# A gated mix of softmax attention and memory attention: the factors of the octets are made by GpSimd with a power and a Newton step instead of by VectorE's reciprocal

## Chip, cores and metric

One Trainium2 chip, one core. The metric is the device time of one execution in microseconds (us). The kernel before took 1857.35 us, the median of three runs (1856.53 to 1861.13).

## What is computed

Two attentions over the same 2048 rows of 512, with 32 heads of 16, mixed by a gate that depends on the row. A is full softmax attention. B works in four segments of 512 rows: causal softmax inside a segment, and a linear memory (a matrix M and a vector z for each head) that holds the segments before.

```python
def reference(A_x, A_wqkv, A_wo, B_x, B_wq, B_wk, B_wv, B_wo, B_beta, gate_w):
    # A
    scores = jnp.einsum("bhqd,bhkd->bhqk", q, k) * scale
    p = _softmax(scores, axis=-1)
    o = jnp.einsum("bhqk,bhkd->bhqd", p, v)
    a = o.transpose(...).reshape(B, S, D) @ wo
    # B, for each segment s
    logits = jnp.einsum("bhqd,bhkd->bhqk", qs, ks) * scale + mask
    a_dot = jnp.einsum("bhqk,bhkd->bhqd", _softmax(logits, axis=-1), vs)
    num = jnp.einsum("bhld,bhde->bhle", pq, M)
    den = jnp.einsum("bhld,bhd->bhl", pq, z)[..., None] + 1e-6
    o = g * (num / den) + (1.0 - g) * a_dot
    M = M + jnp.einsum("bhld,bhle->bhde", pk, vs)
    z = z + jnp.einsum("bhld->bhd", pk)
    # mix
    g = _sigmoid((x * gate_w).sum(-1, keepdims=True))
    return g * a + (1 - g) * b
```

## The kernel before

A first stage, some 330 us long, projects queries, keys and values of both sides, stores them in DRAM, makes the memory parts of B (numerators `numd`, denominators `dend`) and begins the maxima. The main loop that follows is the place of the change.

The work of the main loop is cut into units. A unit is one side, a group of four heads (`g`, eight groups) and a chunk of 512 queries (`c`, four chunks). An A unit takes 64 slots and a B unit 10; the two kinds alternate, so that a pair takes 74 rounds of the loop, and in what follows "a unit" is such a pair of 74 rounds. One round `n` does this, in the order in which it is written, which is the order on every engine:

- things due at this round (`at`, `beside`): loads, and the steps of the octets
- `score_part(n)` (line 640): one 50x128 by 50x512 product of keys and queries on TensorE into one of three PSUM banks `st`, and its exponential on ScalarE (line 663) into `p`. The diagonal blocks of B are zeroed by GpSimd (line 644).
- `max_part(n + 96)`: the same kind of product (line 196) for a slot 96 rounds ahead, into one of four PSUM banks `sm`, and the maximum over its 512 keys on VectorE (line 211; for B with a mask, line 221, one or two pieces). When a unit's maxima are complete, GpSimd splits them into two parts `ms` (lines 178 and 179), TensorE transposes those eight to twelve rounds later (line 187), and SyncE puts them beside the queries (line 193), where the score product subtracts them.
- every third round: products of `p` and the values (line 696, up to three pieces of 128 queries, four or five when the queue of pieces is long) into the bank `ops`, or, for finished chunks, sixteen output products at a time (line 773).

With the values a column of ones is multiplied, so that row 16 of each head's result is the softmax sum. A finished unit is stored to DRAM (`od`, line 701). When two units of a side are stored, their eight heads are an octet, and `octet` divides them by their sums and multiplies them by the gate. Its four steps are due at rounds `t0`, `t0 + 10`, `t0 + 17` and `t0 + 28`:

- `load`: SyncE fetches the 8 x 512 sums as a tile `rec` of 128x32 (line 737) and the values (line 744).
- `factors`: VectorE makes the reciprocal (line 747) and multiplies it by the gate (line 751), for side B also by one less the memory's share `ogh` in the same instruction (line 749). SyncE sends the 128x32 factors to DRAM (line 752).
- `factor`: SyncE fetches them back, spread over the 16 dims of each head, as `inv` of 128x512 (line 756).
- `scale`: GpSimd multiplies the values by `inv` (line 759), and for B from the second chunk on adds the scaled memory part (line 761).

There are three kinds of octets: A and B (16 each), and M, the memory part of B (12, from the second chunk on), whose sums are `dend`. The last octet, A of the last chunk, is handled after the loop with `vector=True`: its scale is VectorE's, since everything waits for it. The instructions of SyncE, GpSimd and VectorE run in the order of the program, each engine waiting by itself.

Of the kernel before, what the change touches and what calls it, by code (L numbers as in the profile page):

```python
# [10 lines left out]
F32 = mybir.dt.float32  # L11
F32R = mybir.dt.float32r
AF = mybir.ActivationFunctionType
ALU = mybir.AluOpType
# [31 lines left out]
def gated_mix(ctx, tc, x, xT, wqkv, a_wo, b_wq, b_wk, b_wv, b_wo, beta, gate_w, out):  # L46
    nc = tc.nc
# [35 lines left out]
    ogh = const.tile([128, NO], F32, name="ogh")  # L83
# [26 lines left out]
    for k in range(NU):  # L110
# [4 lines left out]
        for p in range(64 + 10 * len(bs)):  # L115
            r = (len(maxs) + 1) % 2
# [456 lines left out]
    gate = {(s, c): gp.tile([128, 32], F32, name=f"g{s}{c}") for s in "AB" for c in range(NCH)}  # L573
# [6 lines left out]
    fr = ctx.enter_context(tc.tile_pool(name="fr", bufs=1, reuse_waits="tile"))  # L580
# [132 lines left out]
    def heads(rows):  # L713

        return rows.unsqueeze(0).broadcast_to([DH, 8, CH])

    held = {}
    scaled = set()

# [3 lines left out]
    def at(n, f):  # L723
        beside.setdefault(n, []).append(f)

    def octet(side, o, c, t0, vector=False):

        hs = slice(8 * o, 8 * o + 8)
        sums, rows, eng = (dend[c][hs], rdM[c][hs], nc.gpsimd) if side == "M" else (od[side, c][hs, 16], rd[side, c][hs], nc.gpsimd)
        if vector:  # L730
            eng = nc.vector
        k = {}

        def load():
            assert side == "M" or {(side, 2 * o, c), (side, 2 * o + 1, c)} <= stored
            k["rec"] = fr.tile([128, 32], F32, tag="rec", name="rec", bufs=3)
            nc.sync.dma_start(k["rec"], sums.rearrange("h (q t) -> h q t", q=16))
            if side == "M":
                k["v"] = held["M", c, o] = fr.tile([128, CH], F32, tag="vM", name="vM", bufs=2)
            else:  # L740
                if (side, c) not in held:
                    held[side, c] = fr.tile([128, NO, CH], F32, tag="v" + side, name="v" + side, bufs=2)
                k["v"] = held[side, c][:, o]
            nc.sync.dma_start(k["v"], numd[c][:, o] if side == "M" else od[side, c][hs, 0:16].rearrange("h r t -> r h t"))

        def factors():
            nc.vector.reciprocal(k["rec"], k["rec"])  # L747
            if side == "B":
                nc.vector.scalar_tensor_tensor(k["rec"], k["rec"], ogh[:, o:o + 1], gate["B", c], op0=ALU.mult, op1=ALU.mult)
            else:  # L750
                nc.vector.tensor_mul(k["rec"], k["rec"], gate["A" if side == "A" else "B", c])
            nc.sync.dma_start(rows.rearrange("h (q t) -> (h q) t", q=16), k["rec"])

        def factor():
            k["inv"] = fr.tile([128, CH], F32, tag="inv", name="inv", bufs=3)
            nc.sync.dma_start(k["inv"], heads(rows))

        def scale():
            eng.tensor_mul(k["v"], k["v"], k["inv"])
            if side == "B" and c:  # L760
                eng.tensor_add(k["v"], k["v"], held.pop(("M", c, o)))
            scaled.add((side, o, c))
        for n, f in ((0, load), (10, factors), (17, factor), (28, scale)):
            if t0 is None:
                f()
            else:
                at(t0 + n, f)
# [113 lines left out]
    for b in range(4):  # L881
# [3 lines left out]
        t = fr.tile([128, D], F32, tag="vM" if b % 2 else "res", name="res", bufs=2)  # L885
# [4 lines left out]
def build():  # L890
    import concourse.bacc as bacc
    nc = bacc.Bacc("TRN2", target_bir_lowering=False, num_devices=1)
    shapes = {"x": (S, D), "xT": (D, S), "wqkv": (D, 3 * D), "a_wo": (D, D), "b_wq": (D, D), "b_wk": (D, D),
              "b_wv": (D, D), "b_wo": (D, D), "beta": (H,), "gate_w": (D,)}
    args = [nc.dram_tensor(n, s, F32, kind="ExternalInput").ap() for n, s in shapes.items()]
    out = nc.dram_tensor("out", (S, D), F32, kind="ExternalOutput").ap()
    with tile.TileContext(nc) as tc:
        gated_mix(tc, *args, out)
    return nc
# [23 lines left out]
```

## Time and profile before

| | |
|---|---|
| median of three runs | 1857.35 us |
| the profiled execution | 1856.77 us, span 1855.0 us |
| TensorE, matmul rows | 1846.4 us, 17769 instructions |
| VectorE | 1609.3 us (87% of the span), 3417 instructions |
| ScalarE | 1446.3 us (78%) |
| GpSimd | 236.6 us (13%), 387 instructions |
| granted TensorE clock | 1.000 |

In the profile PE is TensorE's matmul, PEld its weight load, DVE VectorE, ACT ScalarE, POOL GpSimd, SPq the queue of SyncE, which issues most DMAs. A group's row holds the line, engine, operation, output<-inputs, shapes and count; after the bar the busy time and the mean ns of one; after the second bar the engine's idle time just before, and what ended it. A row of the order of time holds start, length, engine, line, operation, and in brackets the idle time before it and what ended it. A row of the waits holds who waited for whom, the total in us, how often, and the longest.

### The profile page before, as it was taken

How to read it: one execution, taken by the hardware profiler on the slowest of the kernel's cores; microseconds unless marked ns; L12 is line 12 of the kernel's file. 1: busy time of each engine (PE TensorE's matmuls, PEld its weight loads, DVE VectorE, ACT ScalarE, POOL GpSimd, SP SyncE). 2: the span in 40 equal slices, each digit the busy share in tenths (PEclk: the TensorE clock that was granted, in tenths of full speed). 3: DMA queues.
4: the chain of work that ended last, by engine and by line, in shares of the span. 5: the costliest groups of instructions: out<-in, count | busy, mean ns of one | idle time of the engine just before them, and what ended most of it. 6: DMA issues, size and time to landing. Idle time of an engine off the chain costs nothing.

```text
span 1855.0 us, 45914 instructions
## 1 busy us (share of the span) xinstructions
PE 1846.4 (100%) x17769; PEld 987.1 (53%) x17769; DVE 1609.3 (87%) x3417; ACT 1446.3 (78%) x2772; POOL 236.6 (13%) x387
## 2 busy tenths in 40 slices
PE   9999999999999999999999999999999999999999
PEld 7888676555555554444444444444444455555446
DVE  4234678999999999999999999999999999999920
ACT  5445444888888888888888888888888888888884
POOL 3001222001010101010101010101010100111120
PEclk9999999999999999999999999999999999999999
DMA  7568645345343433454434343434343433433321
GB/s 238 191 232 257 203 170 189 116 110 135 88 112 88 113 88 112 103 115 103 115 99 117 100 111 104 113 103 115 103 115 103 115 105 99 117 102 97 93 65 48
DMA packets 124169, 227.28 MB, mean 123 GB/s; under 512 B 34952, under 2 KB 49960, under 8 KB 123440
## 3 DMA queue, kind: packets, MB, share of 16 engines
q1 hardware_dynamic: 122448, 222.68, 42.6%
q8 instruction: 141, 2.31, 0.5%
q0 software_dynamic: 1216, 1.14, 0.2%
q14 instruction: 76, 0.62, 0.1%
q10 hardware_dynamic: 288, 0.52, 0.1%
HBM read 155.52 MB, written 67.52 MB: 120 GB/s over the span
## 4 chain that ended last, share of the span: by engine, by line
PE 94%; DVE 2%; DMA 1%; ACT 1%; POOL 1%; issue 0%; SPq 0%; POOLq 0%; DVEq 0%
PE ops L696 32%; PE st L640 28%; PE sm L196 15%; PE pr L294 11%; PE ops L773 6%; PE sm L773 1%; DVE pm L211 1%; POOL mn L354 1%; PE num L476 1%; DMA raw<-xT 0%; PE mt_ps L187 0%; DMA qdB<-q 0%; PE mps L507 0%; DMA raw<-wqkv 0%; ACT ex L361 0%
## 5 line engine op out<-in xcount | busy, mean ns | idle before, releaser
L663 ACT ACTIVATE p<-st 128x512 f32<-128x512 f32 x2304 | 1210.8, 601 | 207.0 <-PE sm L196 164.4
L211 DVE TENSOR_REDUCE pm<-sm 128x1 f32<-128x512 f32 x2048 | 1264.5, 682 | 14.3 <-PE sm L196 13.7
L196 PE MATMUL sm<-kA,qA 48*128 48x512 f32 x2048 | 737.6, 446 | 0.2 <-DVE pm L211 0.2
L640 PE MATMUL st<-qA,kA 50*128 50x512 f32 x2048 | 678.8, 433 | 0.0
L640 PEld LDWEIGHTS st<-qA,kA 50*128 50x128 f32 x2048 | 334.1, 185 | 423.8 <-ACT p L663 367.8
L696 PE MATMUL ops<-p,vA 128*17 128x512 f32 (+3 forms) x5848 | 556.4, 469 | 0.0
L196 PEld LDWEIGHTS sm<-kA,qA 48*128 48x128 f32 x2048 | 332.9, 184 | 29.6 <-DVE pm L211 11.0
L221 DVE CUSTOM_DVE_ANT_0 rest<-sm,mask 128x128 f32<-128x128 f32 (+3 forms) x512 | 248.3, 485 | 7.5 <-PE sm L196 0.8
L696 PEld LDWEIGHTS ops<-p,vA 128*17 128x17 f32 x5848 | 109.7, 95 | 180.9 <-issue 163.2
L196 PE MATMUL sm<-kB,qB 48*128 48x128 f32 (+3 forms) x512 | 149.3, 352 | 0.0
L644 POOL TENSOR_SCALAR_AFFINE_SELECT p<-p 128x512 f32<-128x512 f32 x128 | 79.5, 637 | 465.4 <-ACT p L663 461.1
L357 DVE TENSOR_TENSOR q<-full,q 128x512 fp32r<-128x512 f32 x64 | 44.4, 694 | 88.3 <-ACT q L350 87.5
L640 PE MATMUL st<-qB,kB 50*128 50x384 f32 (+3 forms) x512 | 114.1, 337 | 0.0
L640 PEld LDWEIGHTS st<-qB,kB 50*128 50x128 f32 x512 | 71.6, 185 | 60.8 <-ACT p L663 56.7
L196 PEld LDWEIGHTS sm<-kB,qB 48*128 48x128 f32 x512 | 86.1, 185 | 7.3 <-DVE pm L211 2.9
L696 PE MATMUL ops<-p,vB 128*17 128x128 f32 (+3 forms) x1192 | 86.5, 398 | 0.0
L349 ACT COPY full<-pr 128x512 f32<-128x512 f32 x64 | 37.4, 584 | 52.5 <-PE pr L294 52.1
L178 POOL CAST ms<-pm 128x16 fp32r<-128x16 f32 x32 | 6.3, 198 | 511.5 <-DVE pm L221 511.5
L747 DVE RECIPROCAL rec<-rec 128x32 f32<-128x32 f32 x44 | 15.2, 344 | 64.7 <-DMA rec<-odA 34.5
L773 PE MATMUL ops<-woA,vA 128*32 128x128 f32 x1664 | 66.9, 278 | 0.0
L773 PE MATMUL ops<-woB,vB 128*32 128x128 f32 x1664 | 64.6, 273 | 0.0
L294 PE MATMUL pr<-xh,wql 128*128 128x512 f32 x128 | 54.4, 425 | 0.3 <-ACT xh L407 0.2
(144 smaller groups left out, 1401.0 us busy)
## 6 DMA issues: line engine op xcount, KB each, us to landing
kA<-kdA SPq DMA_DIRECT2D x256, 128.0 KB
vA<-vdA SPq DMA_DIRECT2D x31, 544.0 KB
kA<-kdA SPq DMA_DIRECT2D x256, 64.0 KB
qdA<-q SPq DMA_DIRECT2D x32, 256.0 KB
kdA<-q SPq DMA_DIRECT2D x32, 256.0 KB
qdB<-q SPq DMA_DIRECT2D x32, 256.0 KB
qA<-qdA SPq DMA_DIRECT2D x64, 128.0 KB
kdB<-q SPq DMA_DIRECT2D x32, 256.0 KB
```

Source lines behind the costliest of these rows:

```text
L196: nc.tensor.matmul(ps[:, n0:n0 + n], rows(qt[u][:, :, s * 128:(s + 1) * 128], h, 48), rows(k[:, :, k0:k0 + n], h, 48), start=True, stop=True)
L211: nc.vector.tensor_reduce(pm[:, h, s, kc:kc + 1], ps, axis=AX.X, op=ALU.max)
L221: nc.vector.tensor_tensor_reduce(out=tri["rest"][:, 0:w], in0=ps[:, n0:n0 + w], in1=tri["mask"][:, CH - w:], scale=-1.0, scalar=3.0e38, op ...
L294: nc.tensor.matmul(ps, l(a, k), r(b, k), start=(n == 0), stop=(n == 11))
L349: nc.scalar.copy(full, ps)
L354: nc.gpsimd.tensor_scalar_min(ph["mn"], full, 0.0)
L357: nc.vector.tensor_sub(q2, full, q1.bitcast(F32))
L640: nc.tensor.matmul(ps[:, n0:n0 + CH - q0], rows(k[:, :, b * 128:(b + 1) * 128], h, 50), rows(q[:, :, q0:], h, 50), start=True, stop=True)
L644: nc.gpsimd.affine_select(out=x, in_=x, pattern=[[0, 4], [1, 128]], base=0, channel_multiplier=-1, compare_op=ALU.is_ge, fill=0.0)
L663: nc.scalar.activation(p[:, h], ps, AF.Exp, scale=SCALE)
L696: nc.tensor.matmul(ops[32 * h:32 * h + 17, q0:q0 + 128 * w], v[:, 17 * h:17 * h + 17], p[:, h, c0:c0 + 128 * w], start=(i == 0), stop=done ...
L773: nc.tensor.matmul(ps[32 * t:32 * t + 32, 128 * (j % (ps.shape[1] // 128)):128 * (j % (ps.shape[1] // 128)) + 128], held[side, c][:, o, 12 ...
```

## The change

For every octet but the last one GpSimd makes the factors: a constant tile `minus` of -1 is set once, `rec` to the power of -1 is taken into `rcp`, and one Newton step corrects it: `err` = 2 - `rec` x `rcp`, `rec` = `rcp` x `err`. Then come the multiplications by `ogh` (B alone, now an instruction of its own) and by the gate. The last octet keeps VectorE's reciprocal and multiplication. Two tiles of 128x32 with two buffers each and the constant are added to the pool `fr`. The rounds at which the steps are due, the DMAs and all other instructions stay as they were.

```diff
+    minus = fr.tile([128, 32], F32, name="minus")
+    nc.gpsimd.memset(minus, -1.0)
     held = {}
     scaled = set()
...
         def factors():
-            nc.vector.reciprocal(k["rec"], k["rec"])
+            rec = k["rec"]
+            if vector:
+                eng.reciprocal(rec, rec)
+            else:
+
+                r, e = (fr.tile([128, 32], F32, tag=t, name=t, bufs=2) for t in ("rcp", "err"))
+                eng.tensor_tensor(r, rec, minus, op=ALU.pow)
+                eng.tensor_mul(e, rec, r)
+                eng.tensor_scalar(e, e, -1.0, 2.0, op0=ALU.mult, op1=ALU.add)
+                eng.tensor_mul(rec, r, e)
             if side == "B":
-                nc.vector.scalar_tensor_tensor(k["rec"], k["rec"], ogh[:, o:o + 1], gate["B", c], op0=ALU.mult, op1=ALU.mult)
-            else:
-                nc.vector.tensor_mul(k["rec"], k["rec"], gate["A" if side == "A" else "B", c])
+                eng.tensor_scalar_mul(rec, rec, ogh[:, o:o + 1])
+            eng.tensor_mul(rec, rec, gate["A" if side == "A" else "B", c])
             nc.sync.dma_start(rows.rearrange("h (q t) -> (h q) t", q=16), k["rec"])
```

## Prediction

> **What bounds the kernel now.** I read the page's head first, for the span against which everything is counted.
>
> ```profile
> span 1855.0 us, 45914 instructions
> ```
>
> TensorE shows as busy all through on that page, but its ends are modelled, so its busy share can't tell whether it works or waits. The next view is the waits, which can.
>
> ```profile
> DVE pm L211 <- PE sm L196: 13.7, 18, 2.4
> ...
> PEld sm L196 <- DVE pm L211: 13.9, 52, 0.6
> ```
>
> In the whole run VectorE stands for a max product 18 times, and TensorE's weight load is seen standing for VectorE's release of a bank 52 times. Both are small, so the two engines run at nearly the same pace, with four banks between them. Which one sets the pace has to be read stage by stage. The kernel offers an experiment of its own: units (74 rounds: 64 of A, 10 of B) alternate between kinds that differ in their octets. In the first chunk the even units hold an A and a B octet, the odd ones none. I put window edges at the starts of the max products that are issued in each unit's first round. Columns: stretch, length, busy time of PE, PEld, DVE, ACT, POOL with counts, clock, DMA.
>
> ```profile
> 420.50:468.30 47.80, 47.59 (x468) 24.19 (x467) 47.25 (x103) 40.57 (x80) 6.18 (x11) 1.00 0.49 132
> 468.30:513.60 45.30, 45.30 (x465) 23.96 (x461) 44.98 (x97) 39.26 (x77) 3.12 (x9) 1.00 0.30 88
> 513.60:561.10 47.50, 47.50 (x462) 24.21 (x461) 47.11 (x102) 40.06 (x79) 5.82 (x11) 1.00 0.41 110
> 561.10:607.60 46.50, 46.50 (x470) 23.67 (x469) 46.19 (x99) 40.55 (x80) 3.59 (x10) 1.00 0.33 90
> 607.60:654.30 46.70, 46.70 (x465) 24.32 (x461) 46.31 (x101) 39.42 (x77) 5.62 (x11) 1.00 0.44 109
> 654.30:700.20 45.90, 45.90 (x461) 23.74 (x460) 45.58 (x98) 39.78 (x78) 3.23 (x9) 1.00 0.33 89
> ```
>
> VectorE is busy all but 0.2 to 0.6 us of each unit, and its busy time follows the length. Three units with octets take 142.0 us, three without 137.7: one pair of octets costs 1.43 us of elapsed time. TensorE's work is the same in both kinds, and its clock is 1.00. So in this stage VectorE is the bound. In the second and third chunks odd units hold one M octet (the memory part), even ones an A and a B octet:
>
> ```profile
> 748.40:794.40 46.00, 46.00 (x442) 20.53 (x438) 45.64 (x99) 39.10 (x78) 4.08 (x9) 1.00 0.38 95
> 794.40:841.60 47.20, 47.20 (x473) 21.52 (x470) 46.81 (x102) 40.61 (x79) 7.41 (x12) 1.00 0.51 113
> 841.60:888.70 47.10, 47.10 (x495) 21.44 (x491) 46.75 (x101) 40.55 (x79) 4.82 (x11) 1.00 0.41 101
> 888.70:935.10 46.40, 46.40 (x442) 21.10 (x438) 46.02 (x101) 39.20 (x78) 6.77 (x11) 1.00 0.48 117
> 935.10:981.90 46.80, 46.80 (x472) 20.97 (x470) 46.45 (x100) 40.59 (x79) 4.77 (x10) 1.00 0.40 100
> 981.90:1029.50 47.60, 47.60 (x497) 21.94 (x493) 47.22 (x103) 40.59 (x79) 7.44 (x13) 1.00 0.50 120
> ```
>
> Sums: 139.9 us with M, 141.2 us with A and B, so 0.43 us a unit for one octet more. In the last chunk units three apart (the same place in the bursts of three rounds) can be compared: the first and third rows hold M, AB; so do the fourth and the second.
>
> ```profile
> 1497.60:1545.70 48.10, 48.10 (x633) 25.22 (x630) 47.09 (x100) 40.90 (x80) 4.88 (x10) 1.00 0.35 100
> 1545.70:1594.20 48.50, 48.50 (x593) 23.84 (x589) 47.50 (x103) 40.86 (x80) 7.41 (x13) 1.00 0.43 120
> ...
> 1641.30:1689.50 48.20, 48.20 (x633) 25.49 (x630) 47.19 (x102) 41.16 (x80) 7.40 (x12) 1.00 0.43 112
> 1689.50:1738.00 48.50, 48.50 (x592) 23.30 (x588) 47.44 (x97) 41.13 (x80) 4.86 (x11) 1.00 0.37 98
> ```
>
> An octet more costs 0.1 us (48.2 against 48.1) and 0.0 (48.5 twice). VectorE idles 1 us a unit here: TensorE, with more value and output products, sets the pace.
>
> **What is removed.** Of 44 octets 43 lose their two VectorE instructions: 16 A less the last, 16 B and 12 M, four of a kind in each chunk and M from the second chunk on.
>
> ```profile
> L747 DVE RECIPROCAL rec<-rec 128x32 f32<-128x32 f32 x44 | 15.2, 344 | 64.7 <-DMA rec<-odA 34.5 <-DMA rec<-dend 23.4 <-DMA rec<-odB 6.9
> L749 DVE SCALAR_TENSOR_TENSOR rec<-rec,ogh,gB 128x32 f32<-128x32 f32 x16 | 4.9, 308 | 0.6
> L751 DVE TENSOR_TENSOR rec<-rec,gA 128x32 f32<-128x32 f32 x16 | 3.1, 192 | 0.5
> ```
>
> Durations overlap, so I take what the pair displaces from the order of time on VectorE:
>
> ```profile
> 991.39 0.34 DVE L747 RECIPROCAL rec<-rec 128x32 f32<-128x32 f32 x1
> 991.76 0.19 DVE L751 TENSOR_TENSOR rec<-rec,gA 128x32 f32<-128x32 f32 x1
> 991.87 1.88 DVE L211 TENSOR_REDUCE pm<-sm 128x1 f32<-128x512 f32 x3
> ```
>
> From 991.39 to 991.87: 0.48 us for A or M, with the next maximum right behind. For B I add the longer second instruction (308 - 192 ns): 0.60 us. A pair A and B is 1.08 us, with an M 1.56 us.
>
> **The sum.** First chunk, four pairs (the last of them falls into the unit after the six shown): 4 x 1.08 = 4.3 us by VectorE's work, 4 x 1.43 = 5.7 us by the units' difference (a burst held by the reciprocals may also starve VectorE afterwards). I take 5.0. Second and third chunk, eight pairs and eight M: the units give back 0.43 us for 0.60 us of work, a share of 0.72; 8 x 1.56 x 0.72 = 9.0 us. Bounds: 12.5 us if every us counts, 0 if TensorE is the bound at the first relief. The share must fall as VectorE's load does, so I take 8.5. Last chunk, three pairs and three M before the maxima end: 4.7 us of work at a share of 0.1, that is 0.5 us (bounds 0 and 4.7). M and B of the last pair come after VectorE's last maximum and hide behind TensorE. Together 14.0 us (bounds 4.3 and 22.9).
>
> **What is added.** GpSimd gets five instructions of 128x32 an octet, six for B, and one constant of -1 at the start. Multiplications are bounded by two rows of its own:
>
> ```profile
> L759 POOL TENSOR_TENSOR vB<-vB,inv 128x512 f32<-128x512 f32 x16 | 20.5, 1283 | 30.9 <-DMA inv<-rdB 30.9
> ...
> L179 POOL TENSOR_TENSOR ms<-pm,ms 128x16 fp32r<-128x16 f32 x32 | 7.1, 223 | 2.6
> ...
> L354 POOL TENSOR_SCALAR mn<-full 128x512 f32<-128x512 f32 x24 | 36.3, 1512 | 102.3 <-ACT full L349 82.0 <-DVE jk L441 20.4
> ```
>
> Between 16 and 512 elements a straight line gives 0.26 us for 32; with a wait for the one before it I count 0.3 us. The power has no row. From below it is 0.26 us, from above by the longest row 1.5 us; being a function and no single step, it is nearer the upper one, and I take 1.5. An A or M octet is then 2.7 us of GpSimd, a B octet 3.0.
>
> This is free only while it hides. The tightest place is a B octet of the second or third chunk; from SyncE's, GpSimd's and TensorE's order of time:
>
> ```profile
> 998.76 0.61 SPq L737 DMA_DIRECT2D rec<-odB  x1
> ```
>
> ```profile
> 1007.64 0.20 POOL L178 CAST ms<-pm 128x16 fp32r<-128x16 f32 x1 [8.36 <-DVE pm L221]
> ```
>
> ```profile
> 1014.18 0.39 PE L187 MATMUL mt_ps<-identf,ms 128*32 128x128 f32 x4
> ```
>
> The sums are fetched at 998.76 and, by the last octet B below, land 2.2 us later, at 1001.0. GpSimd idles from 999.28 to 1007.64, when it must split the maxima, and TensorE needs the split at 1014.18. Queued behind the factors on GpSimd are this split, then the octet's scale; in other octets the diagonals of B. So 6.6 us lie free before the split and 6.0 more (after its 0.5) before TensorE notices: a power of up to 6.6 + 6.0 - 1.5 = 11.1 us costs nothing. SyncE sends the factors away and has loads queued behind that; so far it stood there for VectorE, which comes to the reciprocal behind its maxima, while GpSimd is free when the sums land. So I expect no new wait on its queue and count no gain.
>
> In the closing stretch nothing hides in VectorE, so the slower chain is seen bare:
>
> ```profile
> 1802.31 0.65 SPq L737 DMA_DIRECT2D rec<-odB  x1
> ```
>
> ```profile
> 1804.51 0.35 DVE L747 RECIPROCAL rec<-rec 128x32 f32<-128x32 f32 x1 [6.89 <-DMA rec<-odB]
> ```
>
> ```profile
> 1812.33 1.28 POOL L761 TENSOR_TENSOR vB<-vB,vM 128x512 f32<-128x512 f32 x1
> ```
>
> ```profile
> 1832.68 18.48 PE sm L773 x672
> ```
>
> That octet is scaled at 1813.6; 2.4 us more (3.0 for 0.6) moves it to 1816. Its output products are the last but 16 groups of the 18.48 us that begin at 1832.68, so some 17 us are spare. The very last octet stays on VectorE: nothing.
>
> **A rule against it.** VectorE's maxima beside GpSimd's 43 scales of 1.28 us show no stretch: the longest of 2048 is 693 ns against a median of 681.
>
> ```profile
> L211 DVE TENSOR_REDUCE pm<-sm x2048: 668/681/693, 190.3 to 1772.7; 128x1 f32<-128x512 f32 x187
> ```
>
> The Trainium skill (Perfetto Trace Analysis, Optimizing Scalar/DVE Operations) warns that GpSimd and VectorE share an SBUF read port, so that moving work between them might not help. The trace speaks against it for these maxima, which read PSUM; by the rule alone the sum would turn into the loss of the third rival.
>
> **The rivals.** (1) TensorE is the bound from the second chunk on as soon as VectorE is relieved. For it: the units there have only 0.3 to 0.4 us of VectorE idle and TensorE more products; against: 0.43 us for one octet more. Only the first chunk gains, 5 us: 1852 us. (2) The power is long, and GpSimd's split comes late to TensorE, which is in order. It decides from 11.1 us a power; 15 B octets pay the rest, and past 11.1 + 14/15 = 12.0 us the kernel is slower. At 14 us: 15 x 2.9 = 44 lost, 14 gained, 1887 us. For it: no row prices a power; against: the factor of seven over the longest row. (3) VectorE is locked out while GpSimd works: 27 x 2.7 + 16 x 3.0 = 121 us added less 23 removed, 1955 us; the 693 ns speak against it. That the change doesn't do what it says is excluded: in the instruction lists of the two programs TensorE's order is the same, VectorE's loses 86 and GpSimd's grows by 232.
>
> **How the numbers follow.** The profiled run took 1856.77 us (span 1855.0); less 14.0 that is 1842.8. The median of the three is 0.58 higher, so 1843 us. Chances: forecast 0.66, TensorE as bound 0.14, a long power 0.14, the lock 0.03, small unforeseen losses 0.03. The forecast's own range is 1835 (all 22.9 us) to 1851. I extend it to 1858, which takes in the first rival and leaves out the slow ones. 0.3%, what a measurement can tell, is 5.6 us, so faster begins under 1851.8: the forecast and a share of 0.04 of the first rival, 0.70; within, 0.12; slower, 0.18.
>
> **What would show it.** VectorE keeps one reciprocal. Units of the first chunk become equal, near 45.9 us; those of the second and third fall from 46.85 to about 46.3 on average; those of the last stay. VectorE's waits for max products grow, GpSimd's new instructions start some 2 us after the fetch of the sums, and the split of maxima keeps its wait for VectorE. The forecast is wrong if the power's row exceeds 11 us, if maxima beside GpSimd take over 0.70 us, or if the middle units stay at 46.8 with VectorE idle more.

## The result, and the profile after

The changed kernel takes 1847.78 us (median of five, 1846.10 to 1849.58) against 1857.34 us (five runs, 1856.38 to 1861.13) of the kernel before: a ratio of 0.9946, with an interval of 0.9935 to 0.9957. That is 9.6 us faster; the prediction's sum was 14.0. The direction and the range held, the forecast gain was half as much again as the measured one. In the changed kernel the lines behind the factors are ten higher (759 is now 769, and so on).

Where the 8.9 us between the two profiled spans (1855.0 and 1846.1) come from is seen in three stretches of the main loop, cut at the same rounds in both kernels: units 1 to 8 (the first chunk's octets), 9 to 24 (second and third chunk), 25 to 29 (last chunk). Columns as in the prediction's windows; first the kernel before:

```profile
374.70:748.40 373.70, 373.49 (x3657) 189.46 (x3657) 370.63 (x794) 319.82 (x618) 37.09 (x74) 1.00 0.39 107
748.40:1497.60 749.20, 749.20 (x7436) 340.42 (x7434) 743.02 (x1600) 640.73 (x1247) 93.49 (x160) 1.00 0.43 107
1497.60:1737.90 240.30, 240.30 (x3022) 122.19 (x3018) 235.21 (x497) 203.63 (x397) 28.52 (x51) 1.00 0.38 105
```

and the changed one:

```profile
375.90:744.00 368.10, 368.10 (x3656) 187.00 (x3655) 365.65 (x778) 319.39 (x618) 89.89 (x118) 1.00 0.39 108
744.00:1489.00 745.00, 745.00 (x7437) 332.14 (x7434) 739.63 (x1552) 640.75 (x1247) 250.29 (x288) 1.00 0.42 108
1489.00:1729.30 240.30, 240.30 (x3024) 121.90 (x3020) 233.81 (x483) 203.73 (x397) 74.28 (x88) 1.00 0.38 105
```

The first chunk gives 5.6 us, the two middle ones 4.2, the last none. The first stage ends 1.2 us later (375.9 against 374.7) and the rest after the last stretch takes 0.3 us less; over the profiles of the kernels below that leave the first stage as it is, its end lies between 374.0 and 376.2 us, so these are not put down to the change.

The units of the first chunk that hold an A and a B octet, 47.8, 47.5 and 46.7 us before, are now like the units three places away that hold none (46.5, 45.9 and 45.3 us):

```profile
421.70:468.20 46.50, 46.50 (x468) 23.69 (x467) 46.18 (x99) 40.56 (x80) 19.39 (x22) 1.00 0.48 136
...
513.50:559.40 45.90, 45.90 (x461) 23.76 (x460) 45.58 (x98) 39.78 (x78) 18.90 (x22) 1.00 0.43 113
...
605.90:651.20 45.30, 45.30 (x465) 23.91 (x461) 44.98 (x97) 39.26 (x77) 18.89 (x22) 1.00 0.44 113
```

In the second chunk (units 9 to 14) the even ones, with A and B, lose 0.4 to 0.6 us, and the odd ones, with M, stay where they were:

```profile
744.00:789.90 45.90, 45.90 (x440) 20.22 (x438) 45.58 (x97) 39.15 (x77) 10.56 (x14) 1.00 0.37 95
789.90:836.70 46.80, 46.80 (x473) 20.79 (x470) 46.48 (x98) 40.62 (x79) 20.56 (x23) 1.00 0.46 114
836.70:883.90 47.20, 47.20 (x497) 21.32 (x493) 46.88 (x99) 40.65 (x79) 11.36 (x16) 1.00 0.42 101
883.90:929.70 45.80, 45.80 (x439) 20.13 (x438) 45.45 (x97) 39.06 (x77) 19.70 (x22) 1.00 0.46 117
929.70:976.50 46.80, 46.80 (x471) 20.78 (x469) 46.48 (x98) 40.62 (x79) 11.34 (x15) 1.00 0.39 101
976.50:1023.70 47.20, 47.20 (x497) 21.23 (x493) 46.88 (x99) 40.60 (x79) 20.64 (x24) 1.00 0.47 121
```

Both kinds now take the same time at the same place of the burst cycle (three units apart): 45.9 and 45.8, 46.8 twice, 47.2 twice. Read the VectorE column too (the third pair). The first unit lost an M octet's two instructions, 0.48 us, and VectorE is busy 45.58 us instead of 45.64. A maximum lasts 0.68 us but in a row they begin 0.60 us apart (three in 1.88 us, in the prediction's rows), so two records overlap. When VectorE waits a little before each, the overlap can shrink and the busy time stay. So its share need not tell whether VectorE is the bound; a pair of runs below shows it.

The groups of the page show the price of the power:

```profile
L755 POOL TENSOR_TENSOR rcp<-rec,minus 128x32 f32<-128x32 f32 x43 | 234.1, 5444 | 182.0 <-DMA rec<-dend 138.3 <-DMA rec<-odB 22.4 <-DMA rec<-odA 21.2
```

5.44 us, where the prediction took 1.5 and held 1.5 for the upper bound. What stands behind it on GpSimd in the B octet that the prediction looked at, in order of time:

```profile
996.74 5.43 POOL L755 TENSOR_TENSOR rcp<-rec,minus 128x32 f32<-128x32 f32 x1 [2.97 <-DMA rec<-odB]
...
1003.70 0.25 POOL L761 TENSOR_TENSOR rec<-rec,gB 128x32 f32<-128x32 f32 x1
1003.90 0.20 POOL L178 CAST ms<-pm 128x16 fp32r<-128x16 f32 x1
...
1004.68 0.22 POOL L179 TENSOR_TENSOR ms<-nm,ms 128x16 fp32r<-128x16 f32 x1
```

```profile
1008.35 0.39 PE L187 MATMUL mt_ps<-identf,ms 128*32 128x128 f32 x4
```

The split of the maxima now begins right behind the factors: GpSimd no longer stands for VectorE's maxima there. The split ends at 1004.90, and TensorE transposes it 3.4 us later. It is late on GpSimd and still in time on TensorE.

### The profile page after: what moved, and what is told of

It is laid out like the page before. It is cut to its first block, busy times and chain, and to the rows that moved or that the text cites. A ratio compares the mean times of both kernels' runs of the same rounds, so it can differ in the third digit from the quotient of the medians.

```text
span 1846.1 us, 46034 instructions
## 1 busy us (share of the span) xinstructions
PE 1836.3 (99%) x17769; PEld 975.1 (53%) x17769; DVE 1597.8 (87%) x3331; ACT 1445.7 (78%) x2772; POOL 518.4 (28%) x619
## 4 chain that ended last, share of the span: by engine, by line
PE 95%; DMA 2%; ACT 1%; DVE 1%; POOL 1%; issue 0%; SPq 0%; POOLq 0%; DVEq 0%; ACTq 0%
PE ops L696 32%; PE st L640 29%; PE sm L196 14%; PE pr L294 10%; PE ops L783 6%; PE sm L783 1%; POOL mn L354 1%; DMA raw<-xT 1%; PE num L476 1%; DMA vs<-wqkv 0%; DMA qdB<-q 0%; PE mt_ps L187 0%; DMA raw<-wqkv 0%; PE mps L507 0%; ACT full L349 0%
## 5 line engine op out<-in xcount | busy, mean ns | idle before, releaser
L755 POOL TENSOR_TENSOR rcp<-rec,minus 128x32 f32<-128x32 f32 x43 | 234.1, 5444 | 182.0 <-DMA rec<-dend 138.3
L354 POOL TENSOR_SCALAR mn<-full 128x512 f32<-128x512 f32 x24 | 36.3, 1512 | 102.1 <-ACT full L349 81.8
L178 POOL CAST ms<-pm 128x16 fp32r<-128x16 f32 x32 | 6.3, 198 | 204.1 <-DVE pm L221 204.1
```

The costliest lines, as they stand in the source:

```text
L354: nc.gpsimd.tensor_scalar_min(ph["mn"], full, 0.0)
L755: eng.tensor_tensor(r, rec, minus, op=ALU.pow)
```

## Experiments

Two theories for the missing 4.3 us of the middle chunks: **floor** (TensorE has a least time for a unit there, and the units with M had reached it already) and **GpSimd** (the long power gives the gain back through late splits, scales or loads). Against floor stood **line**, the prediction's own share of 0.72 for each us of VectorE's work.

### M given back to VectorE, and M alone moved

```diff
-            if vector:
+            eng = nc.vector if side == "M" or vector else nc.gpsimd
+            if vector or side == "M":
```

> The changed kernel with the 12 M octets given back to VectorE (reciprocal and multiplication, 0.48 us each). Theory floor: from the second chunk on TensorE has a least time for a unit, which the units with an M octet had already reached, so their 0.48 us hides; odd units of the second and third chunk stay at 45.9, 46.8 and 47.1 us and the time at 1847.8 us, within 1. Theory line (the prediction's share of 0.72): the eight odd units grow by 0.35 us, 2.8 us in all, 1850.6 us.

The other way round, only M moved:

```diff
-            if vector:
+            eng = nc.gpsimd if side == "M" else nc.vector
+            if side != "M":
...
-                eng.tensor_scalar_mul(rec, rec, ogh[:, o:o + 1])
-            eng.tensor_mul(rec, rec, gate["A" if side == "A" else "B", c])
+                eng.scalar_tensor_tensor(rec, rec, ogh[:, o:o + 1], gate["B", c], op0=ALU.mult, op1=ALU.mult)
+            else:
+                eng.tensor_mul(rec, rec, gate["A" if side == "A" else "B", c])
```

> The kernel before with only the 12 M octets moved to GpSimd; A and B stay on VectorE as before. Theory floor: no gain, 1857.3 us within 1. Theory line: 8 x 0.35 = 2.8 us gained, 1854.5 us.

With M on VectorE: 1847.76 us (ratio to before 0.9947, 0.9934 to 0.9961). With M alone on GpSimd: 1857.42 us (0.9997, 0.9989 to 1.0006). The middle stretch of each (one profile each), first M on VectorE, then M alone moved:

```profile
743.30:1488.80 745.50, 745.50 (x7436) 334.46 (x7434) 739.82 (x1568) 640.73 (x1247) 198.32 (x248) 1.00 0.41 108
```

```profile
748.20:1496.70 748.50, 748.50 (x7436) 337.98 (x7434) 742.63 (x1584) 640.77 (x1247) 144.56 (x200) 1.00 0.41 108
```

Against 745.0 and 749.2 us: eight M octets, 3.84 us of VectorE's work, are worth 0.5 us when A and B are gone and 0.7 us when they are there. A share of 0.13 to 0.18, not 0.72: line falls. And VectorE's busy time with the 3.84 us more is 739.82 us against 739.63: a busy share of 99% on both sides of a difference in work that the time hardly notices.

### The factors left out

```diff
-            else:
-
-                r, e = (fr.tile([128, 32], F32, tag=t, name=t, bufs=2) for t in ("rcp", "err"))
-                eng.tensor_tensor(r, rec, minus, op=ALU.pow)
-                eng.tensor_mul(e, rec, r)
-                eng.tensor_scalar(e, e, -1.0, 2.0, op0=ALU.mult, op1=ALU.add)
-                eng.tensor_mul(rec, r, e)
-            if side == "B":
-                eng.tensor_scalar_mul(rec, rec, ogh[:, o:o + 1])
-            eng.tensor_mul(rec, rec, gate["A" if side == "A" else "B", c])
+            if vector:
+                eng.tensor_mul(rec, rec, gate["A", c])
```

> The changed kernel without the computation of the factors for 43 octets: the bare sums go through the same DMAs and scales, so GpSimd loses 282 us of work and VectorE gets none. Theory floor: the same time as the changed kernel, 1847.8 us within 1. Theory GpSimd (the long power delays the split of maxima, the scales or SyncE's queue, and took back what the sum missed): the missing 4 to 5 us come back, 1843.3 us.

1847.32 us (0.9946, 0.9934 to 0.9959), the same as the changed kernel. Its middle stretch:

```profile
742.90:1488.10 745.20, 745.20 (x7438) 332.37 (x7434) 739.60 (x1552) 640.69 (x1248) 93.27 (x160) 1.00 0.43 108
```

GpSimd is busy 93 us instead of 250, and the stretch takes 745.2 us against 745.0. The power takes nothing back; theory GpSimd falls.

### TensorE's products taken out, and more of VectorE's work

```diff
+    between = {k: v for k, v in between.items() if k[2] == last}
     del between["A", NG - 1, last]
```

> The changed kernel without the output products that run between the scores for the first two chunks (these rows of out stay unwritten); TensorE loses 64 small products a unit in the second and third chunk, VectorE nothing. Theory floor: the units there fall to VectorE's own 45.9 us, 0.65 us each, 1837.5 us. If VectorE or ScalarE or the DMAs make the time there, nothing changes, 1847.8 us.

1839.13 us (two runs; 0.9897, 0.9866 to 0.9928). The middle stretch:

```profile
744.10:1477.80 733.70, 730.79 (x5812) 313.97 (x5810) 728.66 (x1552) 628.76 (x1230) 249.45 (x288) 1.00 0.42 107
```

733.7 us, 45.9 a unit: the units fall by 0.7 us to what the first chunk's take. So what the edit leaves out made the difference. By the trace that is some 124 product instructions a unit on TensorE (2020 of line 783 in the middle stretch before, 32 now; the expectation says 64), and with them one copy a unit on ScalarE (line 807, 0.37 us) and its store. The fall of 0.7 us is more than the copy, but ScalarE's part, and that of the stores, was not separated; that TensorE alone makes the floor is argued.

Now less for VectorE. First, four of a unit's 64 maxima of A read only half of their keys:

```diff
-            nc.vector.tensor_reduce(pm[:, h, s, kc:kc + 1], ps, axis=AX.X, op=ALU.max)
+            nc.vector.tensor_reduce(pm[:, h, s, kc:kc + 1], ps[:, 0:256] if i in (9, 25) else ps, axis=AX.X, op=ALU.max)
```

> The changed kernel with four of a unit's 64 maxima of A taken over the first 256 of their 512 keys (the rest is left out of the maximum; the subtracted value changes, the softmax does not). VectorE loses 4 x 0.27 = 1.07 us a unit, TensorE nothing. Theory floor: units of the first chunk fall from 45.9 towards 44.8 us, those of the second and third stay at 45.9, 46.8, 47.1: 8.5 us gained, 1839 us. Theory line: the latter gain 0.72 x 1.07 each as well, 12 us more, 1827 us.

1835.16 us (two runs; 0.9876, 0.9845 to 0.9906). The first two stretches:

```profile
374.00:734.80 360.80, 360.66 (x3658) 179.12 (x3657) 358.18 (x779) 319.12 (x619) 90.11 (x118) 1.00 0.41 110
734.80:1476.00 741.20, 741.20 (x7438) 327.10 (x7434) 726.49 (x1551) 640.37 (x1248) 250.02 (x288) 1.00 0.43 109
```

8 x 1.07 = 8.6 us of work gave 7.3 in the first chunk; 16 x 1.07 = 17.1 us gave 3.8 in the middle. The floor is soft, a share of 0.22, and not the hard one of the theory; the total lies between its 1839 and line's 1827.

Then a version that leaves nothing out: the last step of A's maxima, the negated maximum over four, is made by GpSimd.

```diff
-            nc.vector.tensor_reduce(nm, pm, axis=AX.X, op=ALU.max, negate=True)
+            d = mp.tile([128, 4, 4, 2], F32, tag="d", name="d")
+            nc.gpsimd.tensor_sub(d, pm[:, :, :, 2:4], pm[:, :, :, 0:2])
+            nc.gpsimd.tensor_scalar(d, d, 0.0, None, op0=ALU.max)
+            nc.gpsimd.tensor_add(d, d, pm[:, :, :, 0:2])
+            nc.gpsimd.tensor_sub(nm, d[:, :, :, 1], d[:, :, :, 0])
+            nc.gpsimd.tensor_scalar(nm, nm, 0.0, -1.0, op0=ALU.max, op1=ALU.mult)
+            nc.gpsimd.tensor_sub(nm, nm, d[:, :, :, 0])
```

> The changed kernel with the last step of A's maxima (negated maximum of four, VectorE, one a unit) also made by GpSimd, in six small instructions. It frees VectorE of some 0.32 us a unit (0.14 us of its own and a 0.19 us wait for the maximum before it). Theory floor: only the eight units of the first chunk gain, 8 x 0.32 = 2.6 us, 1845.2 us; later units stay. Theory line: the 16 units after them gain 0.72 x 0.32 each as well, 6.3 us, 1841.5 us. If GpSimd's longer chain before the split comes late to TensorE, units with A and B octets grow instead.

1846.00 us (1845.57 to 1846.27; 0.9936, 0.9924 to 0.9949), the lowest of the versions that leave nothing out. The first two stretches:

```profile
376.30:741.90 365.60, 365.60 (x3656) 186.29 (x3655) 363.93 (x770) 319.38 (x618) 101.63 (x166) 1.00 0.39 109
741.90:1486.10 744.20, 744.20 (x7438) 330.81 (x7434) 739.18 (x1536) 640.66 (x1247) 273.90 (x384) 1.00 0.42 108
```

2.5 us less in the first chunk, 2.6 expected; 0.8 us in the middle. Against the changed kernel the whole run's 1.8 us lie inside the two intervals; the stretches of one profile show the gain, the totals alone do not.

### How much longer the power could have been

```diff
+                for _ in range(1):
+                    eng.tensor_tensor(e, rec, minus, op=ALU.pow)
                 eng.tensor_tensor(r, rec, minus, op=ALU.pow)
```

> The changed kernel with the power taken twice in a row (the first result is overwritten), 10.9 us of powers an octet. By the prediction's point of 11.1 us a power this is still free: 1848 us, within 2. If the queue behind the power has less room than worked out, the units with A and B octets grow.

> The power taken three times, 16.3 us an octet. By the prediction's rival 15 B octets pay 16.3 - 11.1 = 5.2 us each, 78 us, 1926 us. If the late split is taken up by something not counted (GpSimd starts earlier, TensorE has room elsewhere), well under 1870 us.

Twice: 1954.53 us (1.0518, 1.0486 to 1.0551). Three times, with `range(2)`: 2187.48 us (1.1772, 1.1711 to 1.1832). Each is two runs. The prediction's 11.1 us is wrong by far. With the power twice, in the first unit with octets, from SyncE's and TensorE's order of time:

```profile
450.89 0.34 SPq L764 DMA_DIRECT2D rdB<-rec  x1
...
453.13 0.42 SPq L156 DMA_DIRECT2D kB<-kdB  x1
```

```profile
458.12 0.44 PE L196 MATMUL sm<-kB,qB 48*128 48x128 f32 x1 [7.12 <-DMA kB<-kdB]
```

SyncE stands until GpSimd has finished B's factors, which themselves stood behind A's; the next unit's keys are queued behind that DMA and come 7.1 us late. The waits of that run:

```profile
PEld mt_ps L187 <- POOL ms L179: 38.7, 20, 7.4
...
PE sm L196 <- DMA kB<-kdB: 32.9, 9, 7.7
```

Both paths are there: late keys, and late splits. But the wait is not all that it costs. The granted clock (the last column but two) around the standstill of 451 to 458 us:

```profile
451.00:453.50 2.50, 0.00 (x1) 0.00 (x0) 1.00 (x2) 0.88 (x2) 1.81 (x5) 1.00 0.36 98
453.50:463.80 10.30, 5.68 (x38) 2.54 (x38) 3.23 (x8) 2.43 (x5) 0.40 (x1) 0.50 0.96 240
463.80:470.00 6.20, 6.20 (x63) 3.09 (x58) 5.51 (x13) 5.03 (x10) 0.87 (x1) 1.00 0.54 150
```

Some 2.5 us after TensorE stopped its clock fell to a half, and it stayed there for 10.3 us, of which TensorE worked 5.7: another 2.8 us lost. An estimate for the whole loop, in windows of 1 us: TensorE is idle 65 us longer than in the changed kernel, and its busy time times the missing part of the clock is 44 us. Together that is 109 us, where the spans differ by 107. With the power three times it is 231 and 123 us, where they differ by 343.5. In the changed kernel the clock is 1.00 all through the loop.

Where the edge lies was tried with plain products on GpSimd:

```diff
+    pad = fr.tile([128, CH], F32, name="pad")
+    nc.gpsimd.memset(pad, 0.0)
...
                 eng.tensor_tensor(r, rec, minus, op=ALU.pow)
+                for _ in range(1):
+                    eng.tensor_mul(pad, pad, pad)
```

> The changed kernel with one useless product of 128x512 on GpSimd (1.28 us) in each of the 43 octets, so 6.7 us where the power is 5.44. Theory queue (what the doubled power showed: in the first chunk the A and the B octet stand one behind the other on GpSimd, and SyncE's queue holds the next unit's loads behind B's factors; there B's factors left at 450.9 and TensorE stood 7.1 us for keys of B, so about 443.8 is still free, and the changed kernel sends them at 441.0): 2 x 1.28 = 2.6 us later is just free, 1848 us, within 1.5. By the prediction's point of 11.1 us a power: free.

> Two such products, 2.6 us an octet, 8.0 us in place of 5.44. Theory queue: B's factors leave 5.1 us later, 2.4 us too late, in three or four units of the first chunk: 7 to 10 us lost, 1855 to 1858 us, all of it in those units. By the prediction's point of 11.1 us a power: free, 1848 us.

One: 1847.41 us (0.9944, 0.9929 to 0.9959), free. Two, with `range(2)`: 1858.3 us (0.9999, 0.9988 to 1.0010; the runs spread from 1851.71 to 1862.45), the whole gain gone. The first two stretches of the latter, its wait for keys, and the clock around the longest standstill:

```profile
374.40:746.70 372.30, 369.31 (x3656) 185.78 (x3655) 366.38 (x778) 320.02 (x619) 105.91 (x134) 1.00 0.39 107
746.70:1499.30 752.60, 747.96 (x7436) 331.91 (x7434) 740.05 (x1552) 640.74 (x1247) 298.23 (x336) 1.00 0.42 107
```

```profile
PE sm L196 <- DMA kA<-kdA: 5.7, 3, 3.5
```

```profile
833.10:839.90 6.80, 5.21 (x24) 1.63 (x24) 2.48 (x7) 1.58 (x3) 1.26 (x1) 0.50 0.38 116
839.90:845.00 5.10, 5.10 (x60) 2.79 (x60) 4.37 (x11) 4.06 (x9) 0.65 (x1) 1.00 0.00 0
```

The edge lies between 6.7 and 8.0 us, as worked out from the queue. The loss was expected in the first chunk alone, though; it got 4.2 us there and 7.6 in the middle, where keys of A, which also stand behind the factors, came late. By the same estimate as above TensorE stood 4.6 us of the middle stretch, and the half clock behind that took 2.6.

```diff
-            nc.sync.dma_start(rows.rearrange("h (q t) -> (h q) t", q=16), k["rec"])
+            (nc.sync if vector else nc.gpsimd).dma_start(rows.rearrange("h (q t) -> (h q) t", q=16), k["rec"])
...
-            nc.sync.dma_start(k["inv"], heads(rows))
+            (nc.sync if vector else nc.gpsimd).dma_start(k["inv"], heads(rows))
```

> The power taken twice (10.9 us), but the factors leave and come back on GpSimd's own DMA queue, so SyncE's loads are not queued behind them. Theory queue: the units of the first chunk with octets, 54 to 56 us with the doubled power, return to within 1 us of 45.9, and those of the second and third with A and B (52 to 59 us) to under 49; total under 1870 us. Theory GpSimd (its occupancy alone makes the split of maxima late): near 1954 us as before.

2008.91 us (two runs; 1.0813, 1.0791 to 1.0835), worse than the power twice on SyncE's queue. The waits for keys are gone and those for the split have grown; beside them, GpSimd's order of time in the first unit:

```profile
PEld mt_ps L187 <- POOL ms L179: 131.8, 32, 9.7
...
PE mt_ps L187 <- POOL ms L179: 114.4, 23, 9.4
```

```profile
441.78 0.55 POOL L768 DMA_DIRECT2D inv<-rdA  x1 [3.31 <-DMA rdA<-rec]
```

GpSimd now stands 3.3 us for its own factors to land before it may begin B's power, and the split behind that is later still. That run has both DMAs on the other queue and one more wait in GpSimd's order, so it doesn't price SyncE's queue by itself; it shows that the queue is not the only path at this length.

## Why the prediction was right, and where it was not

**The first chunk: right.** VectorE is the bound there (with half maxima, 8.6 us less of its work, 7.3 us came); 5.0 us were taken, between 4.3 and 5.7, and 5.6 came. The units became equal as forecast, at 45.9 us on average. Why a pair of octets is worth 1.4 us when its instructions displace 1.08 was not tried.

**The middle chunks: right in kind, too large.** This is the term that failed: "the units give back 0.43 us for 0.60 us of work, a share of 0.72", applied to all 12.5 us. 8.5 us were taken and 4.2 came. The share was measured between units with M and units with A and B, and then continued below the units with M. There it bends. M's 0.48 us was nearly free (a share of 0.13 to 0.18 by the two runs with M), and so is what is taken from VectorE beyond (0.22 with half maxima). Only A and B, the part above, paid: 749.2 to 745.5 us, 3.7 of their 8.6 us. The units were to fall to about 46.3 us on average and fell to 46.6. So a part of the first rival, TensorE as the bound from the second chunk on, held: not from the first us, but from the level of the M units on. The remark that the share must fall was there, with too small a step.

What misled was the difference between two kinds of unit, "0.43 us for one octet more", set against the first rival as though it went on below the lighter kind. VectorE's small idle time there, 0.3 to 0.4 us a unit, could give no warning. The Trainium skill (Perfetto Trace Analysis, Identifying the Most-Contended Engine) names the busiest engine as the one to improve, by occupancy (the share of time that it is busy), which for VectorE is "also a fair measure of how close you are to roofline", the most that the hardware can do. This trace differs: 739.8 and 739.6 us busy for 3.84 us of difference in work.

**The last chunk: right.** 0.5 us was taken, 0.0 came. VectorE doesn't set the pace there; that TensorE does was not tried.

**The work on GpSimd: right that it hides, wrong in price and in room.** The power is 5.44 us, 3.6 times the estimate; "from above by the longest row 1.5 us" was no bound, since a row of one multiplication says nothing about a function. The other instructions were near the estimate: B's five behind the power take 1.8 us where 1.5 were counted. The split did not keep its wait for VectorE, as the prediction had it (511.5 us over the run before, 204.1 after), and that alone cost nothing: without the factors it waits 505.4 us again, in the same time. The room was wrong as well: not 11.1 us but between 6.7 and 8.0, because "I expect no new wait on its queue" left out that in the first chunk A and B stand one behind the other on GpSimd while SyncE holds the next keys behind B's factors. SyncE stands 126 us in all at the issue of the factors in the changed kernel, and stood 80 before. That the two errors did not show in the time is luck: 5.44 is below 6.7; with 2.6 us more in each octet the kernel would have been no faster than before. The second rival had the right mechanism as one of two paths, at too late a point: at 10.9 us, where it promised no loss, the kernel lost 107 us, some 40% of it by the half clock behind each standstill, which the prediction didn't price.

**The lock: right that it isn't seen.** With 282 us of additional work on GpSimd the longest of 2048 maxima is 693 ns, as before. The median is 683 ns against 681, and it is 683 without the factors too, so that is not the added work's doing:

```profile
L211 DVE TENSOR_REDUCE pm<-sm x2048: 669/683/693, 191.5 to 1763.5; 128x1 f32<-128x512 f32 x187
```

## What to carry to other kernels

When two engines run at nearly one pace, what a saved us is worth bends: compare units that differ in work, but don't continue the line below the lightest unit seen. A busy share near one, of an engine whose records overlap, doesn't show that it is the bound; take a little work off or put some on, and look at the length of the units. Work that is moved to an idle engine is free only as long as everything queued behind it, on that engine and on the DMA queue that waits for its result, still comes in time; find the edge of both before counting on it. And price what comes late by more than its wait: look at the granted clock behind the standstill.

## What the runs showed of the hardware

A power of 128x32 elements on GpSimd takes 5.44 us, 21 times a product of the same size (0.25 us).

After some 2 to 2.5 us without work TensorE's granted clock was 0.50 in the two standstills looked at, and it stayed so until 5 to 6 us after the work had begun again (453.5 to 463.8 us with the power twice, 833.1 to 839.9 with two products more).

The middle stretch of sixteen units takes 745.0 us in the changed kernel, 745.2 without the factors and 745.0 with one product more on GpSimd, while whole runs of one kernel spread by 3 us and more; stretches cut at the same rounds resolve edits that the totals cannot.
